# Sets of quarter-array matmuls placed one behind the other on TensorE, two pauses in the planner, and later batches planned two steps sooner

## The chip, the cores and the metric

The kernel runs on one core of one Trainium2 chip. The metric is the device time of one execution in microseconds (us), as the median of several runs; a profiled execution comes with a trace of every instruction. TensorE is called PE in the profile, VectorE DVE, ScalarE ACT, GpSimd POOL and SyncE SP; SP issues the DMAs.

## The reference

The input is `x` of 8 batches x 3136 tokens x 256 channels, with a filter of 1569 frequencies and two weight matrices of a two-layer product.

```
X = rfft(x, axis=1);  y = irfft(X * filter)               # along the 3136 tokens
mixed = real(fft(fft(y, axis=1), axis=2))                 # along tokens and channels
u = y + mixed
un = (u - mean(u)) / sqrt(var(u) + 1e-6)                  # along the channels
out = u + relu(un @ w_ch1) @ w_ch2                        # 256 -> 1024 -> 256
```

## The kernel before

All transforms are matrix products. A batch goes through these stages, each in seven parts: a first forward stage (`first_pair`, for batches 2 to 7), a second forward stage with the filter (`spectrum`), a transpose by DMA, a first inverse stage (`inverse1`), and a second inverse stage (`inverse2`), whose rows go to DRAM (`dy`) and come back in groups of 256 rows (`fetch`). For each of the 49 groups `prepare` mixes channels and normalizes, and `products` makes the two weight products. Numbers are kept as pairs of float16, so most products are three matmuls. One "step" is an eighth of a group: one piece of the first product (`h`, six matmuls of 512 columns, L1564) and two halves of the second (`acc`, six matmuls of 256 columns each, L1604), with everything else threaded between. There are 392 steps, and they keep TensorE in work from about 95 us to the end.

Three kinds of work use the array as four quarters of 64 x 64, each quarter with its own rows and its own output partitions, so that four matmuls run side by side. They are called sets here: an **s set** (`first_pair`, L671), an **i set** (`inverse1`, L1075, with L1066 in a batch's first part) and a **y set** (`inverse2`, L1198). A set takes two of the four PSUM banks of the ring `psf`; `spectrum` and `mixing` take one bank of the same ring each. All other matmuls use the whole array.

The order of all instructions on every engine is fixed when the kernel is built, by a planner (`Plan`). Each piece of work is a Python generator that yields an engine, an assumed length in us and, if wanted, a key; the planner keeps a clock of its own, lines the pieces up per engine (`line_up`) and, when an engine comes free (`run`), takes the one with the lowest key. On the chip the engines follow that order and wait on semaphores, so a piece that the planner thought ready and that is late holds up its engine. A "gate" at t lets a piece go on when step t - 4 is done (`gate`, L1283). Keys are in steps: the first product of step q has key q, the second q + 2.5. The s set has key t - 6 (`BOOST`, L667), the y set t - 8 (L1187), the i set t itself (L1062).

The scale of a batch (`weigh_x`, L610 to L626) is a maximum over measures of the seven pieces of `x` (L600, ScalarE, each after its load), a square root on ScalarE (L617), a transpose on TensorE (`pow2`, L470), a few operations on VectorE and a product with ones on TensorE (`spread`, L488). For the i set, `spectrum` ends in a DMA transpose issued by SP (L958), which writes `z`; after it `done("z", ...)` lets `inverse1` go on.

The time of a batch's stages hangs on one number, `brought(b, c)` (L1275), the step at which part c of batch b is wanted:

```python
return 8 * ((b * NS + 224 * c) // 256) - COME - (c == 1) * 2
```

`load_b2` (L1126) brings part c's input back from DRAM at a gate of `brought(b, c) - 3`, and `inverse2` (L1173) is gated at `brought(b, c)`. The main program sets the other stages back from `brought(b, 0)`: `s0` (spectrum) is `brought(b, 0) - 5.2 - 6.5 - 13 * 1.45`, `t0` (first stage) is `s0 - 4.6 - 13 * 1.15`, `x0` (loads of `x`) is `t0 - 8.5`, and the i set of part ch has t = `s0 + 1.45 * (2 * ch + 1) + 6.5`.

Of the kernel before, what the change touches and what calls it, by code (L numbers as in the profile page):

```python
# [26 lines left out]
NS = N // 2  # L27
# [7 lines left out]
COME = 18  # L35
# [4 lines left out]
TWIN = 0.86  # L40
FOURS = 0.85
BOOST = 6
PASSES = ((0, 0), (1, 0), (0, 1))
BACKED = 6.5
RAW_IN = (None, None, "ys", "ys", "ut", None, None, None)
# [20 lines left out]
class Plan:  # L66


    def __init__(self):
        self.now = self.end = self.moved = 0.0  # L70
        self.heap, self.count, self.live = [], 0, 0
        self.queues = {e: [] for e in ("PE", "DVE", "ACT", "POOL", "SP", "calm")}
        self.free_at = dict.fromkeys(self.queues, 0.0)

    def post(self, t, f, *args):
# [11 lines left out]
    def step(self, task, value, issued=None):  # L87
        try:
            what, *rest = task[0].send(value)
        except StopIteration:  # L90
            self.live -= 1
            return
        if issued is not None and what not in ("PE", "DVE", "ACT", "POOL"):
            self.end = issued
        if what in self.queues:
            if len(rest) > 1:
                task[1] = rest[1]
            self.post(self.end + HOP * (task[2] != what), self.line_up, what, task, rest[0])
            task[2] = what
        elif what == "until":  # L100
            self.until(task, list(rest))
        elif what == "take":
            self.post(self.end, self.ask, rest[0], task, *rest[1:])

# [9 lines left out]
    def set(self, event, now=False):  # L114
        end = self.end
        if now:
            self.end = self.now
        event.time = self.end
        for task, events in event.waiting:
            self.until(task, events)  # L120
        self.end = end

    def line_up(self, engine, task, length):
        self.count += 1
# [25 lines left out]
    def run(self):  # L150
        while self.heap:
            self.now, _, f, args = heapq.heappop(self.heap)
            f(*args)
            while self.heap and self.heap[0][0] <= self.now:
                _, _, f, args = heapq.heappop(self.heap)
                f(*args)
            for e, queue in self.queues.items():
                if e == "calm" and queue:
                    e = "SP"
                    if self.moved > self.now + CALM:  # L160
                        self.post(self.moved - CALM, int)
                        continue
                if queue and self.free_at[e] <= self.now:
                    _, _, task, length = heapq.heappop(queue)
                    if e == "SP":
                        issue = TURN if length == 1.65 else ISSUE
                        self.moved = max(self.moved, self.now + issue + REACH) + length
                        self.free_at[e] = max(self.now + issue, self.moved - BACKLOG)
                        self.end = self.moved + LANDED
                    else:  # L170
                        self.end = self.free_at[e] = self.now + length
                    self.post(self.free_at[e], int)
                    self.step(task, None, self.free_at[e] if e == "SP" else None)
        assert not self.live
# [199 lines left out]
def _program(ctx, tc, nc, a, NB):  # L374
# [22 lines left out]
    def give(name, *ks):  # L397
        for k in ks:
            plan.give(rings[name], k)
# [6 lines left out]
    def done(*key):  # L406
        plan.set(ev(*key))
# [55 lines left out]
    def pow2(col, name):  # L463

        rows = col.shape[0]
        ring, bank_ = ("psh", spare) if name in ("x0", "F") else ("psf", bank)
        k = yield take(ring)
        pt = bank_("pt_" + name)
        yield "PE", 0.3
        nc.tensor.transpose(pt[:1, :rows], col, ident[:rows, :rows])  # L470
        yield "DVE", 0.9
        row = tp.tile([1, 2], F32, tag="row", name="row_" + name, bufs=3)
        nc.vector.tensor_reduce(row[:, 0:1], pt[:1, :rows], axis=AX.X, op=ALU.max)
        give(ring, k)
        nc.vector.tensor_scalar(row[:, 0:1], row[:, 0:1], 1e-18, None, op0=ALU.max)
        ri = row.bitcast(I32)
        nc.vector.tensor_scalar(ri[:, 0:1], ri[:, 0:1], EXPO, None, op0=ALU.bitwise_and)
        nc.vector.tensor_scalar(ri[:, 1:2], ri[:, 0:1], EXPO, None, op0=ALU.bitwise_xor)
        return row
# [130 lines left out]
    def weigh_x(b):  # L610
        yield until(*(("mx", b, q) for q in range(7)))
        m = ms[b]
        yield "DVE", 0.2
        nc.vector.tensor_reduce(m[:, 7:8], m[:, 0:7], axis=AX.X, op=ALU.max)
        if b:
            yield "ACT", 0.25
            nc.scalar.activation(m[:, 7:8], m[:, 7:8], AF.Sqrt)  # L617
        row = yield from pow2(m[:, 7:8], f"x{b}")
        if b:
            yield "DVE", 0.3  # L620
            nc.vector.tensor_scalar(row[:, 0:1], row[:, 0:1], 1 / (16 * SMALL), None, op0=ALU.mult)
            nc.vector.tensor_scalar(row[:, 1:2], row[:, 1:2], 16 * SMALL, None, op0=ALU.mult)
        sx = tp.tile([128, 2], F32, tag="sx", name=f"sx_{b}", bufs=3)
        yield from spread(sx, row, f"x{b}")
        sxs[b] = sx
        done("sx", b)  # L626
# [30 lines left out]
    def first_pair(b, q, t):  # L657

        yield gate(t)
        yield until(("sx", b), ("s1q",))  # L660
        if b not in d1s:
            d1s[b] = dp.tile([2, 56, 28, 2, 256], F16, tag="d1", name=f"d1_{b}")
        x = xs[b, q]
        sx = sxs[b][:, 1:2]
        kp = yield take("psf", 2)
        ps = [bank(f"s1_{b}_{q}_{i}").rearrange("p (n c) -> p n c", n=2) for i in range(2)]
        yield "PE", FOURS, t - BOOST  # L667
        for c in range(2):
            for i in range(2):
                row = slice(64 * i, 64 * i + 56)  # L670
                nc.tensor.matmul(  # L671
                    ps[i][64 * c : 64 * c + 64], s1q[row], x[row, 2 * c : 2 * c + 2], start=True, stop=True
                )
        give("big", 21 * b + q - 7)
        kx = yield take("x16")
        odd = fp.tile([128, 2, 256], F32, tag="x16", name=f"odd_{b}_{q}", bufs=3)
        yield "ACT", 0.58
        nc.scalar.activation(odd, ps[1], AF.Copy, scale=sx)
        for out, op in ((ps[1], ALU.subtract), (odd, ALU.add)):
            yield "DVE", 0.73  # L680
            nc.vector.scalar_tensor_tensor(out, ps[0], sx, odd, op0=ALU.mult, op1=op)
        give("psf", kp)
        k = yield take("ast")
        st = fp.tile([128, 2, 2, 2, 256], F16, tag="ast", name=f"ast_{b}_{q}", bufs=3)
        yield "ACT", 0.55
        nc.scalar.copy(st[:, 1, :, 0], ps[1])
        plan.spawn(sum_half(b, q, kx, odd, st), t)
        yield "DVE", 0.66
        nc.vector.tensor_tensor(st[:, 1, :, 1], ps[1], st[:, 1, :, 0], op=ALU.subtract)
        give("psf", kp + 1)  # L690
        yield until(("sum", b, q))
        for c in range(2):
            yield "SP", 0.85
            n = 4 * q + 2 * c
            nc.sync.dma_start(
                d1s[b][:, :, n : n + 2].rearrange("s p n h c -> p s (n h c)"),
                st[64 * c : 64 * c + 56].rearrange("p s n h c -> p s (n h c)"),
            )
        give("ast", k)
        done("d1", b, 2 * q)  # L700
        done("d1", b, 2 * q + 1)
# [153 lines left out]
    def spectrum(b, ch, hf, t):  # L855
# [103 lines left out]
            zs[b, ch][:, :, 128 * hf : 128 * hf + 128], y16.rearrange("p l j q -> p (l j q)")  # L959
        )  # L960
        give(f"y16_{hf}", k)
        done("z", b, ch, hf)

    spectra, mixed = {}, [0]
# [89 lines left out]
    def inverse1(b, ch, t):  # L1054
# [4 lines left out]
        kp = yield take("psf", 2)  # L1059
        ps = [bank(f"i1_{b}_{ch}_{i}").rearrange("p (j c) -> p j c", j=2) for i in range(2)]  # L1060
        z = zs[b, ch].rearrange("p (l j) c -> p l j c", l=2)
        yield "PE", TWIN + 0.5 * (ch == 0), t - 0  # L1062
        if ch == 0:
            for s in range(2):
                for i, (lx, lw) in enumerate(PASSES):
# [3 lines left out]
        for i, (lx, lw) in enumerate(PASSES):  # L1069
            for jj in range(2):  # L1070
                for c in range(ch == jj == 0, 2):
                    e = 4 * ch + 2 * c + jj + 1
# [100 lines left out]
    def inverse2(b):  # L1173
        for c in range(1 - min(b, 1), 7):
            t = urgent(b, c)
# [8 lines left out]
            k, bt = b2s[b, c]  # L1184
            kp = yield take("psf", 2)
            ps = [bank(f"y_{b}_{c}_{o}").rearrange("p (j c) -> p j c", j=2) for o in range(2)]
            yield "PE", TWIN if b else 2 * TWIN, t - 8  # L1187
            passes = PASSES if b else [(0, None)]
            for i, (lx, lw) in enumerate(passes):
                table = i2[:, :, lw] if b else i2f  # L1190
                for js in range(2):
                    for o in range(2):
                        row = slice(64 * o, 64 * o + 56)
                        for h in range(2):
                            e, half, turn = 2 + 2 * h + js, h, js
                            if c == o == 0:
                                e, half, turn = h if js == 0 else 2 + 2 * h, js, h
# [76 lines left out]

    def brought(b, c):  # L1275

        return 8 * ((b * NS + 224 * c) // 256) - COME - (c == 1) * 2

    def urgent(b, c):

# [495 lines left out]
    for b in range(NB):  # L1776
# [23 lines left out]
        for ch in range(7):  # L1800
            for h in range(2):
                t = s0 + half * (2 * ch + h)
                plan.spawn(spectrum(b, ch, h, t), t)
            t = s0 + half * (2 * ch + 1) + 2.2
# [72 lines left out]
```

## Time and profile before

| what | value |
| --- | --- |
| time, three runs | 1388.2 us median (1386.5, 1388.2, 1391.54) |
| profiled execution | 1391.44 us, span 1389.6 us |
| mean granted TensorE clock | 0.992 |
| PE busy | 1354.4 us, 97% of the span |
| DVE, ACT, POOL busy | 72%, 61%, 51% of the span |
| chain that ended last | PE 72%, DMA 8%, DVE 7%, POOL 4%, ACT 4%, issue 3% |

Busy times are shares of the span from the first to the last instruction. In a timeline a row is a run of like instructions: its start, its length, the engine and line, what it writes and reads, and the count. The lengths of neighbouring matmul rows overlap, since matmuls are pipelined; the pace is read from the starts.

### The profile page before, as it was taken

The numbers are of one execution on the slowest core, as the hardware profiler recorded it, in microseconds if no ns is written. First come the engines' busy times: TensorE is split into PE (matmuls) and PEld (weight loads), VectorE is DVE, ScalarE is ACT, GpSimd is POOL, SyncE is SP. The second block draws the span as 40 slices with busy tenths as digits, with TensorE's granted clock in tenths as the row PEclk, the third lists the DMA queues.
The fourth block names the chain that finished last, engine by engine and source line by source line (L and its number), as shares of the span: only waits on it lengthen the run. The fifth ranks groups of instructions, "written<-read, shape, count | busy, mean of one in ns | idle before, by whom it ended". The sixth has DMA issues, their size and how long they took to land.

```text
span 1389.6 us, 33404 instructions
## 1 busy us (share of the span) xinstructions
PE 1354.4 (97%) x12879; PEld 917.6 (66%) x12879; DVE 997.1 (72%) x2162; ACT 845.3 (61%) x1631; POOL 706.4 (51%) x865
## 2 busy tenths in 40 slices
PE   9989999999899999999999999999899999999998
PEld 8845766666657765677656665666566776666666
DVE  6888896788678777678677875777648778465442
ACT  6776567556755677565765667647656565444341
POOL 2713881378536864388443863368614766222210
PEclk9989999999999999999999999999999999999999
DMA  9797998699889897887979797787966986554320
GB/s 259 238 249 209 240 202 208 204 227 205 195 231 238 184 199 192 256 188 185 228 197 217 174 218 182 216 205 170 221 176 180 205 197 168 141 138 105 100 61 31
DMA packets 353603, 265.35 MB, mean 191 GB/s; under 512 B 216188, under 2 KB 290588, under 8 KB 353444
## 3 DMA queue, kind: packets, MB, share of 16 engines
q1 hardware_dynamic: 353444, 263.22, 77.8%
q8 instruction: 101, 1.65, 0.5%
q14 instruction: 58, 0.48, 0.1%
HBM read 113.72 MB, written 99.09 MB: 153 GB/s over the span
## 4 chain that ended last, share of the span: by engine, by line
PE 72%; DMA 8%; DVE 7%; POOL 4%; ACT 4%; issue 3%; SPq 2%; DVEq 0%; POOLq 0%; ACTq 0%
PE acc L1604 29%; PE h L1564 29%; DMA x<-xq 4%; PE s L671 3%; PE y L1198 3%; PE s L890 2%; PE mix L1305 2%; PE i L1075 2%; DMA z<-late 1%; DMA ft<-fiT 1%; ACT xsq L600 1%; DVE h L1593 1%; DMA ft<-frT 1%; POOL eo L1011 1%; POOL late L954 1%
## 5 line engine op out<-in xcount | busy, mean ns | idle before, releaser
L1604 PE MATMUL acc<-w2s,h 128*128 128x256 f16 x4704 | 589.0, 273 | 1.2 <-ACT u L1529 1.0
L1564 PE MATMUL h<-ut,w1s 128*128 128x512 f16 x2352 | 575.6, 381 | 0.2 <-DVE ut L1521 0.2
L1604 PEld LDWEIGHTS <-h 128*128 128x128 f16 x4704 | 449.1, 98 | 138.9 <-issue 24.2
L1593 DVE SCALAR_TENSOR_TENSOR h<-h,h 128x512 f16<-128x512 f32 x392 | 267.8, 683 | 227.1 <-ACT h L1591 225.3
L1591 ACT ACTIVATE h<-h 128x512 f16<-128x512 f32 x392 | 232.8, 594 | 305.6 <-PE h L1564 303.6
L1564 PEld LDWEIGHTS <-w1s 128*128 128x128 f16 x2352 | 225.8, 98 | 205.9 <-issue 14.2
L1535 POOL TENSOR_TENSOR u<-un,u 128x512 f16<-128x512 f32 x92 | 106.4, 1157 | 222.5 <-ACT u L1529 186.5
L1355 POOL TENSOR_TENSOR pages<-sm,pages 128x508 f32<-128x508 f32 x49 | 62.0, 1266 | 107.0 <-ACT sm L1396 66.0
L1507 ACT ACTIVATE un<-pages,sb 128x256 f32<-128x256 f32 x196 | 109.0, 592 | 10.0 <-DVE sb L1454 8.9
L954 POOL TENSOR_TENSOR late<-yt,late 128x448 f16<-128x448 f32 x98 | 102.7, 1052 | 21.2 <-ACT late L952 19.8
L707 POOL TENSOR_TENSOR ast<-odd,ast 128x512 f16<-128x512 f32 x42 | 48.4, 1157 | 123.6 <-ACT ast L705 118.7
L1476 DVE BATCH_NORM_STATS2 st<-pages 128x6 f32<-128x256 f32 x196 | 80.6, 411 | 12.9 <-POOL pages L1361 11.2
L1330 DVE SCALAR_TENSOR_TENSOR pages<-mix,alpha,pages 128x254 f32<-128x254 f32 (+2 forms) x184 | 81.4, 476 | 9.0 <-ACT sm L1396 7.5
L909 DVE SCALAR_TENSOR_TENSOR yt<-s,pF,ft 128x448 f32<-128x448 f32 x98 | 66.0, 674 | 28.1 <-PE s L890 27.0
L1120 POOL TENSOR_TENSOR bt<-sd,bt 128x512 f16<-128x512 f32 x42 | 48.6, 1158 | 70.3 <-ACT bt L1118 70.0
L925 POOL TENSOR_TENSOR yt<-yt,t 128x224 f32<-128x224 f32 x98 | 64.6, 659 | 36.1 <-DVE t L909 33.7
L952 ACT CAST late<-yt 128x448 f16<-128x448 f32 x98 | 54.9, 562 | 40.0 <-POOL yt L927 39.5
L1224 ACT ACTIVATE ys<-y,alpha 128x512 f32<-128x512 f32 x98 | 62.2, 682 | 26.3 <-PE y L1198 22.3
L1618 DVE SCALAR_TENSOR_TENSOR pages<-acc,beta,pages 128x512 f32<-128x512 f32 x98 | 68.6, 741 | 7.3 <-PE acc L1604 7.2
L978 POOL TENSOR_TENSOR ef<-yt 128x224 f32<-128x224 f32 x112 | 72.6, 669 | 0.3
L1011 POOL TENSOR_TENSOR eo<-ef,eo 128x448 f16<-128x448 f32 (+6 forms) x62 | 59.7, 967 | 25.2 <-ACT eo L1007 16.9
L909 DVE SCALAR_TENSOR_TENSOR t<-s,pF,ft 128x448 f32<-128x448 f32 x98 | 65.9, 673 | 0.5 <-POOL yt L927 0.5
(191 smaller groups left out, 1676.6 us busy)
## 6 DMA issues: line engine op xcount, KB each, us to landing
pages<-d SPq DMA_DIRECT2D x112, 224.0 KB
out<-pages SPq DMA_DIRECT2D x98, 256.0 KB
pages<-dy SPq DMA_DIRECT2D x90, 256.0 KB
d<-ast SPq DMA_DIRECT2D x98, 224.0 KB
d<-bt SPq DMA_DIRECT2D x98, 224.0 KB
dy<-ys SPq DMA_DIRECT2D x96, 224.0 KB
x<-xq SPq DMA_DIRECT2D x42, 480.0 KB
at<-d SPq DMA_DIRECT2D x84, 224.0 KB
```

The costliest lines, as they stand in the source:

```text
L909: nc.vector.scalar_tensor_tensor(out, p, pF[:, 1:2], f, op0=ALU.mult, op1=ALU.mult)
L954: nc.gpsimd.tensor_tensor(y16v[:, 1], yh, y16v[:, 0], op=ALU.subtract)
L978: nc.gpsimd.tensor_tensor(eft[:, i], yt[:, 0, i], yt[:, 1, i], op=o)
L1011: nc.gpsimd.tensor_tensor(lo, efv[:, :, e0 : e0 + n], hi, op=ALU.subtract)
L1330: nc.vector.scalar_tensor_tensor(out, p, al, y, op0=ALU.mult, op1=ALU.add)
L1476: nc.vector.bn_stats(st[:, 2 * t + k], y[:, t, k])
L1507: nc.scalar.activation(un[:, k], y[:, t, k], AF.Identity, bias=sb[:, i, 1:2], scale=sb[:, i, 3:4])
L1535: nc.gpsimd.tensor_tensor(u16[:, :, :, 1], unv, u16[:, :, :, 0], op=ALU.subtract)
L1564: nc.tensor.matmul(p.rearrange("p (t k q) -> p t k q", t=2, k=2), w1s[:, d, hw, 128 * f : 128 * f + 128], utv[:, :, :, d, hx], start=i == ...
L1591: nc.scalar.activation(h[:, 0], p, AF.Relu)
L1593: nc.vector.scalar_tensor_tensor(h[:, 1], p, 0.0, h[:, 0], op0=ALU.max, op1=ALU.subtract)
L1604: nc.tensor.matmul(acc[:, kind], h[:, hh, c0 : c0 + 128], w2s[:, f, hw], start=f == 0 and kind == 0 and i == 0, stop=f == 7 and kind == 1 ...
```

## The change

Five edits, all in the planner and in what is yielded to it. No instruction is added or removed.

- The three kinds of sets are lined up in a queue of their own, "quarters", which TensorE serves beside its other queue. When both hold work and the last piece was not a set, the lower key goes first, as before; when the last piece was a set, a set that is lined up goes first whatever its key. A set that follows a set is counted 0.2 us shorter (`MERGED`).
- `weigh_x` waits 1.5 us of planner time before the transpose of the scale is lined up, for batches 2 to 7.
- `spectrum` waits 1 us of planner time behind the DMA transpose, before `z` is called done, for batches 2 to 7.
- For batches 3 to 7 `brought` is two steps lower.
- For the same batches parts 2, 4 and 6 get the `brought` of parts 1, 3 and 5.

```diff
@@ class Plan, __init__, step @@
-        self.queues = {e: [] for e in ("PE", "DVE", "ACT", "POOL", "SP", "calm")}
+        self.queues = {e: [] for e in ("PE", "DVE", "ACT", "POOL", "SP", "calm", "quarters")}
+        self.in_quarters = False
+        elif what == "pause":
+            self.post(self.end + rest[0], self.resume, task, None)
@@ class Plan @@
+    def on_tensor(self):
+
+        whole, quarters = self.queues["PE"], self.queues["quarters"]
+        if whole and quarters and not self.in_quarters:
+            return min(whole, quarters)
+        return quarters or whole
@@ run @@
+                if e == "quarters":
+                    continue
+                if e == "PE":
+                    queue = self.on_tensor()
                 if queue and self.free_at[e] <= self.now:
                     _, _, task, length = heapq.heappop(queue)
+                    if e == "PE":
+                        small = queue is self.queues["quarters"]
+                        length -= MERGED * (small and self.in_quarters)
+                        self.in_quarters = small
@@ weigh_x @@
+        if b > 1:
+            yield "pause", 1.5
         row = yield from pow2(m[:, 7:8], f"x{b}")
@@ first_pair, inverse1, inverse2 @@
-        yield "PE", FOURS, t - BOOST
+        yield "quarters", FOURS, t - BOOST
-        yield "PE", TWIN + 0.5 * (ch == 0), t - 0
+        yield "quarters", TWIN + 0.5 * (ch == 0), t - 0
-            yield "PE", TWIN if b else 2 * TWIN, t - 8
+            yield "quarters", TWIN if b else 2 * TWIN, t - 8
@@ spectrum @@
         give(f"y16_{hf}", k)
+        if b > 1:
+            yield "pause", 1
         done("z", b, ch, hf)
@@ brought @@
-        return 8 * ((b * NS + 224 * c) // 256) - COME - (c == 1) * 2
+        if b > 2 and c:
+            c -= (c - 1) % 2
+        return 8 * ((b * NS + 224 * c) // 256) - COME - (c == 1) * 2 - 2 * (b > 2)
```

## Rows read from the trace of the kernel before

**Rows 1.** The page's part 1: engine, busy us, share of the span, instructions.

```profile
PE 1354.4 (97%) x12879; PEld 917.6 (66%) x12879; DVE 997.1 (72%) x2162; ACT 845.3 (61%) x1631; POOL 706.4 (51%) x865
```

**Rows 2.** Waits of TensorE from 95 us on: total us, times, longest us.

```profile
PE i L1075 <- DMA z<-late: 7.7, 3, 6.4
PE pt_x L470 <- ACT mx L617: 6.5, 4, 2.8
```

**Rows 3.** The timeline of TensorE: the first and the last set.

```profile
79.43 1.09 PE L1198 MATMUL y<-pages,i2f 56*64 56x256 f32 x16
...
1304.70 0.85 PE L1198 MATMUL y<-pages,i2f 56*64 56x256 f16 x24
```

**Rows 4.** The timeline of TensorE, 798 to 809 us: start us, us, work.

```profile
800.26 0.84 PE L1198 MATMUL y<-pages,i2f 56*64 56x256 f16 x22 [0.24 <-DVE t L909]
...
802.77 1.46 PE L1564 MATMUL h<-ut,w1s 128*128 128x512 f16 x6
804.06 0.82 PE L1604 MATMUL acc<-w2s,h 128*128 128x256 f16 x6
...
805.79 1.46 PE L1564 MATMUL h<-ut,w1s 128*128 128x512 f16 x6
807.18 0.85 PE L1075 MATMUL i<-z,late 56*64 56x256 f16 x24
807.96 1.27 PE L1604 MATMUL acc<-w2s,h 128*128 128x256 f16 x10
```

**Rows 5.** The same view around 417 us, where two sets stand together.

```profile
415.82 1.46 PE L1564 MATMUL h<-ut,w1s 128*128 128x512 f16 x6
417.20 1.50 PE L1198 MATMUL y<-pages,i2f 56*64 56x256 f16 x48
418.64 1.48 PE L1604 MATMUL acc<-w2s,h 128*128 128x256 f16 x12
```

**Rows 6.** TensorE's groups by line, first 807.1 us, then first 634.0: xcount, busy, mean ns.

```profile
L1564 PE MATMUL h<-ut,w1s 128*128 128x512 f16 x1254 | 307.5, 381 | 0.2 <-DVE ut L1521 0.2
...
L1564 PE MATMUL h<-ut,w1s 128*128 128x512 f16 x942 | 231.6, 382 | 0.2 <-DVE ut L1521 0.2
```

**Rows 7.** Timelines of SP: the second transposes of the two sets in Rows 4 and 9.

```profile
795.53 1.23 SPq L958 DMA_TRANSPOSE z<-late  x1
...
612.46 1.24 SPq L958 DMA_TRANSPOSE z<-late  x1
```

**Rows 8.** The chain that ended last, around 473 and 998 us: start us, us, what.

```profile
472.94 3.10 DMA z<-late
...
998.37 9.87 DMA z<-late
```

**Rows 9.** The timeline of TensorE, 622 to 636 us.

```profile
631.22 0.85 PE L1198 MATMUL y<-pages,i2f 56*64 56x256 f16 x24
...
634.06 0.85 PE L1075 MATMUL i<-z,late 56*64 56x256 f16 x24
```

**Rows 10.** The page's part 5: the eviction of a y set's two banks.

```profile
L1224 ACT ACTIVATE ys<-y,alpha 128x512 f32<-128x512 f32 x98 | 62.2, 682 | 26.3 <-PE y L1198 22.3
```

**Rows 11.** The timeline of TensorE around 491 us: an i set after its first matmul.

```profile
491.25 0.85 PE L1075 MATMUL i<-z,late 56*64 56x256 f16 x23 [1.49 <-DVE bt L1099]
```

**Rows 12.** Timelines of TensorE, 376 to 381, then 853 to 862 us: scale's transpose.

```profile
378.27 0.26 PE L470 MATMUL pt_x<-ident,mx 120*1 120x120 f32 x1 [1.62 <-ACT mx L617]
...
856.54 0.26 PE L470 MATMUL pt_x<-ident,mx 120*1 120x120 f32 x1 [2.82 <-ACT mx L617]
```

**Rows 13.** Engines by stretch: us, busy of PE, PEld, DVE, ACT, POOL; granted clock, DMA share, GB/s.

```profile
856.67:860.08 3.41, 3.41 (x16) 2.05 (x15) 1.88 (x8) 3.38 (x7) 2.04 (x2) 0.50 0.29 70
1001.90:1008.28 6.38, 0.01 (x1) 0.00 (x0) 4.63 (x11) 4.50 (x10) 4.98 (x6) 0.89 1.05 238
1008.28:1013.68 5.40, 5.40 (x40) 3.32 (x41) 0.00 (x0) 1.15 (x2) 0.00 (x0) 0.50 1.12 290
```

**Rows 14.** The timeline of TensorE, 1001 to 1015 us.

```profile
1008.28 1.49 PE L1075 MATMUL i<-z,late 56*64 56x256 f16 x24 [6.38 <-DMA z<-late]
```

More of the change, by code (lines that the diff above doesn't have):

```diff
@@ L42 @@
 BOOST = 6
+MERGED = 0.2
 PASSES = ((0, 0), (1, 0), (0, 1))
@@ L92, in step @@
             return
-        if issued is not None and what not in ("PE", "DVE", "ACT", "POOL"):
+        if issued is not None and what not in ("PE", "DVE", "ACT", "POOL", "quarters"):
             self.end = issued
```

## The prediction

> **What bounds the kernel now.** I read the page's busy shares first: TensorE is busy for 97% of the span, the next engine for 72% [rows 1]. So the time is TensorE's work plus its waits, and nothing that only relieves another engine shows. Next, the waits of TensorE behind the start-up: two kinds are large, the i set on the DMA that transposes `z` (7.7 us, three times) and the scale's transpose on ScalarE's square root (6.5 us, four times) [rows 2]. Then the timeline, by starts, for what a set costs beyond its own matmuls. Last the granted clock in the stretches right behind the long waits. The last set starts at 1304.70 [rows 3], 85 us ahead of the end, and behind it TensorE has products only; so a stage that ends sooner doesn't by itself end the kernel sooner.
>
> **Sets that follow one another.** A piece `h` takes 1.29 us from its start to the next piece's (802.77 to 804.06) [rows 4]. With an i set behind it, `h` starts at 805.79 and the work after the set at 807.96, 2.17 us: the set costs 2.17 - 1.29 = 0.88 us [rows 4]. Where two y sets stand together it is 418.64 - 415.82 - 1.29 = 1.53 us for both [rows 5], so the second costs 0.65 and a set that joins another saves about 0.23; I use 0.22. There are 42 s sets, 49 i sets, and 55 y sets by the code; counted along the timeline they stand in 124 runs, the first and the last of them in [rows 3], so 22 of the 146 already have a set ahead of them.
>
> How many more will join? s and y sets have keys 6 and 8 steps below their time, under any product's key, so before the change too they went as soon as they were lined up: for them the new queue alone does almost nothing. It is i sets, with key t, that sit in line while their data are there. Example: part 3 of batch 5 has t = 222 - 30.55 + 10.15 + 6.5 = 208.1 and ran when 1254 / 6 = 209 pieces `h` (steps 0 to 208) were done [rows 6], to the step when its key came up. Its second transpose was issued at 795.53 [rows 7]; with the 3.1 us that such a transfer took at 473 us [rows 8] it had landed at 798.6, before the y set of 800.26 [rows 4]. The change would draw it in behind that set. Of the 42 i sets of batches 2 to 7, I count 15 that start at the step of their key like this one, and 9 of these have a set ahead of them in that time.
>
> Others are later than their key though their data are long there. Part 1 of batch 4 (key 174 - 30.55 + 4.35 + 6.5 = 154.3) ran after 942 / 6 = 157 pieces [rows 6], at 634.06, with its transpose issued at 612.46 [rows 7], which lands by 622.4 even with the longest transfer of the chain, 9.9 us [rows 8]. A y set ran at 631.22, and 2 us behind its end this set [rows 9]. What it waited for is a pair of banks; such sets don't join. The same limit meets the second idea: parts 1 and 2, 3 and 4, 5 and 6 of batches 3 to 7 (15 pairs of y sets) now fall due together, but the second needs the other two banks at once. I take 6 of the 15. So 15 joins, 15 x 0.22 = **3.3 us**, with bounds of 5 (1.1 us) and 30 (6.6 us).
>
> The trace shows the eviction as the longer part: ScalarE takes 682 ns for each of a y set's two banks [rows 10], 1.36 us against the 0.88 of the set, and one i set stood for 1.49 us behind its first matmul until VectorE had cleared its second bank [rows 11]. The Trainium skill's page "TensorEngine Tiling (Array Packing)", section Performance Considerations, says that tiling speeds up TensorE but not the emptying of PSUM. It speaks against this change; by it no pair forms beyond those of before, and the sum would lose its 3.3 us.
>
> **The pause before the scale's transpose.** The pause adds no instruction; the transpose, and behind it the product with ones and the first s set, stand 1.5 us later in TensorE's order, with products ahead of them as cover. It takes off up to 1.5 us from each of the four waits: 1.5 each from 1.62 and 2.82 us [rows 12], and the other two, 6.5 - 1.62 - 2.82 = 2.0 together, whole: 5.0 us. Behind the 2.82 us wait the granted clock was 0.50, the level of 1.2 GHz, for 3.41 us in which TensorE was busy throughout [rows 13]; half of that, 1.7, was lost. Behind the 1.62 us wait there is no such stretch. With 1.3 us of it left I count the 1.7 too: **6.7 us** (bounds 0, if each transpose is just as late against its new place, and 6.5 + 1.7 = 8.2).
>
> **The pause behind the transpose of `z`.** Two waits of 1.3 us together go, and 1.0 of the long one, 6.38 us at 1008 [rows 14]: **2.3 us**. The remaining 5.4 us and the clock behind it, 0.50 over 5.40 us of work [rows 13], 2.7 us lost, I leave in: its transfer took 9.87 us [rows 8] while the DMA engines were full (share 1.05) [rows 13], which a pause of 1 us doesn't cover. Bounds 0 and 7.7 + 2.7 = 10.4.
>
> **Two steps sooner.** A step is 173.1 us / 52 = 3.33 us [rows 6]. For batches 3 to 7 the loads of `x`, the s sets, spectra, transposes, i sets and y sets move together by 6.7 us, so they keep their distances; SP issues the same DMAs sooner, ahead of groups' `fetch` and `out` transfers that stay. By the formula the y sets of part 2 move by 12 steps, those of parts 4 and 6 by 10 in most batches, and with them their two loads each and their `dy` stores: part 2's loads now fall just behind the batch's last transposes, where the next batch's `x` loads are. In itself I cost it at nothing, with products as cover.
>
> **New waits.** An i set drawn in ahead of its key gives up slack: some would find `z` still on its way. Without any slack three sets waited 7.7 us in all [rows 2]; the pause covers the short ones. I charge 2.0 us (bounds 0 and, one more wait like the long one, 6.4 us).
>
> **The sum.** -3.3 - 6.7 - 2.3 + 2.0 = -10.3 us. Against the profiled execution's own time, 1391.4, that is 1381.1. The median of the runs is 1388.2, 3.2 lower, in all likelihood with a shorter long wait, of which the sum takes only 1.0; I carry the difference over: **1378 us**. What is late next is TensorE's own work.
>
> **The rivals.** (1) *The sets don't join*, since banks are held: for it the late i sets above, against it the pair at 417 us. Then 5 joins: 1388.2 - 1.1 - 6.7 - 2.3 + 2.0 = 1380. (2) *The waits come back elsewhere*: the planner makes a new order everywhere, and a chain (load of `x`, measure, root) that is late on the chip is late against any place. Only the joins stay: 1388.2 - 3.3 = 1385, no change. For it: two of six batches wait for nothing and one 2.8 us, so lateness scatters. Against it: a fixed pause shortens every wait. (3) *Slower: the sooner loads meet the transposes.* Place: the end of each batch's inverse stage, where the DMA engines are full already [rows 13]. Price of one such wait: 6.4 + 2.7 = 9.1 us. One more of them eats the gain (1387); from two more on it decides: 1378 + 18 = 1396; of seven batches one has it now. The Trainium skill, "Trainium Kernel Development and Optimization", Key Constraints, says that all DMAs share the same 16 engines and interleave; the share of 1.05 agrees.
>
> **How the numbers follow.** About 0.5% (7 us) is what a measurement of this kernel can tell from no change: faster is below 1381.3, slower above 1395.1. The forecast has 0.60 (0.52 of it below 1381.3), rival 1 0.13 (0.08 below), rival 2 0.18 (0.02 below), rival 3 0.09 (0.07 above 1395.1, the rest between). Faster 0.62, same 0.31, slower 0.07. Lowest, with the good bounds: 1388.2 - 6.6 - 8.2 - (10.4 - 3.2) = 1366. At the top the range takes in rival 2 and one more long wait: 1389. Outside lie most of rival 3 and a little of the rest.
>
> **What would show it.** Joins: rows of 48 matmuls y or of y and i next to each other, and fewer than 110 runs. The pause: idle time before L470 below 2 us in all. `z`: no short waits before L1075. Rival 2: the same sum of TensorE's waits under other names. Rival 3: waits of 4 us and more before L1075 or L1198 on a DMA, with a granted clock of 0.50 behind them. I'd be wrong most easily about the number of joins and the long waits.

## The result and the profile after

| | before | after |
| --- | --- | --- |
| median | 1387.99 us (6 runs, 1386.5 to 1391.54) | 1401.09 us (6 runs, 1397.52 to 1405.09) |
| ratio, 95% interval | | 1.0089 (1.0067 to 1.0111) |
| profiled execution, span | 1391.44, 1389.6 us | 1401.35, 1399.6 us |

The change makes the kernel 13 us slower where 10 us of gain were forecast. One run of e3 below, of 2315.57 us, was in a slow state and is left out of e3's median, which would be 1416.8 us with it (the 1417 of later expectations). The page of after begins as that of before [rows 1]: TensorE is busy for 97% of the span, and only 4 us longer in all.

```profile
span 1399.6 us, 33390 instructions
...
PE 1358.3 (97%) x12879; PEld 923.8 (66%) x12879; DVE 1005.3 (72%) x2162; ACT 844.5 (60%) x1631; POOL 706.0 (50%) x865
```

TensorE's waits from 95 us on (total us, times, longest) show what was traded. The scale's transpose (now L489) waits 0.8 us instead of 6.5 [rows 2]: that pause did its work. The i sets (now L1098, with L1089 in a batch's first part) wait for the transposes of `z` 19.8 us in nine waits, instead of 7.7 in three.

```profile
PE i L1098 <- DMA z<-late: 17.5, 7, 4.4
PE i L1089 <- DMA z<-late: 2.3, 2, 2.0
PE y L1221 <- DMA pages<-d: 1.8, 3, 0.8
...
PE pt_x L489 <- ACT mx L636: 0.8, 1, 0.8
```

Behind five of the waits the granted clock is lower, as it was behind two before [rows 13]. By stretch (us, busy of the engines, clock, DMA share, GB/s), each from the end of a wait:

```profile
376.02:380.60 4.58, 4.58 (x38) 3.05 (x39) 2.59 (x7) 2.81 (x6) 1.15 (x1) 0.50 0.76 181
464.53:469.40 4.87, 4.87 (x58) 4.02 (x58) 2.42 (x4) 2.44 (x7) 1.95 (x4) 0.65 1.21 289
505.46:513.73 8.27, 8.27 (x86) 5.09 (x87) 3.89 (x7) 4.35 (x9) 2.88 (x5) 0.79 1.06 217
534.48:537.60 3.12, 3.12 (x33) 2.13 (x34) 0.19 (x1) 1.76 (x4) 3.00 (x5) 0.50 1.13 236
681.40:684.40 3.00, 3.00 (x28) 1.63 (x28) 0.00 (x0) 0.00 (x0) 0.89 (x1) 0.50 1.13 303
```

A clock of 0.50 is the level of 1.2 GHz; the stretches at 0.65 and 0.79 hold work at both levels. Length times the missing share is 2.3 + 1.7 + 1.7 + 1.6 + 1.5 = 8.8 us lost, against 1.7 + 2.7 = 4.4 before. All waits of the view together are 26.5 us against 19.2. Counted along the timeline, sets stand in 118 runs against 124, which saves 6 x 0.22 = 1.3. So waits +7.3, clock +4.4, joins -1.3: +10.4 us; the spans differ by 10.0. The start-up, in which both programs have the same order up to 170 us, took 2.8 us longer in this execution of after; with it the sum is 13.2, and where 3 us were won back I can't say.

**How one of the waits comes about.** After's timeline of SP around 500 us (start us, us, work):

```profile
499.22 2.20 SPq L979 DMA_TRANSPOSE z<-late  x1
```

its timeline of TensorE there:

```profile
500.66 1.47 PE L1629 MATMUL acc<-w2s,h 128*128 128x256 f16 x12
505.46 0.85 PE L1098 MATMUL i<-z,late 56*64 56x256 f16 x24 [3.32 <-DMA z<-late]
```

and the chain that ended last there (start us, us, what):

```profile
499.22 6.11 DMA z<-late
```

The issue of the transpose ends at 501.42. The i set comes to the head of TensorE at 505.46 - 3.32 = 502.14, 0.7 us behind that. The transfer lands at 505.33. The planner put the set behind the end of the *issue*, not behind the landing. The reason is in `step` (L89 to L107 of after):

```python
if issued is not None and what not in ("PE", "DVE", "ACT", "POOL", "quarters"):
    self.end = issued                                   # end of the DMA's issue
...
elif what == "pause":
    self.post(self.end + rest[0], self.resume, task, None)
```

When SP's piece is taken, `run` sets `self.end` to the landing and hands the end of the issue to `step` as `issued`. Before, the generator went straight on to `done("z", ...)` and set the event at the landing. With the pause the next thing it yields is none of the engines in the tuple, so its clock is set back to the end of the issue, and the 1 us runs from there. By the planner's own constants (`REACH` 0.5, length 1.65, `LANDED` 1.5; at most `BACKLOG` 4.5 + 1.5) the landing lies 3.65 to 6.0 us behind the end of the issue. So on the planner's clock the pause calls `z` done 2.65 to 5 us *sooner* than before. The pause of the scale stands behind a piece on ScalarE, where `issued` is None, and does what it says. This is theory I below; the runs test it.

### The profile page after: what moved, and what is told of

Read it like the earlier page. It is cut to its first block, busy times and chain, and to the rows that moved or that the text cites. A ratio compares the mean times of both kernels' runs of the same rounds, so it can differ in the third digit from the quotient of the medians.

```text
span 1399.6 us, 33390 instructions
## 1 busy us (share of the span) xinstructions
PE 1358.3 (97%) x12879; PEld 923.8 (66%) x12879; DVE 1005.3 (72%) x2162; ACT 844.5 (60%) x1631; POOL 706.0 (50%) x865
## 3 DMA queue, kind: packets, MB, share of 16 engines
q8 instruction: 101, 1.65, 0.5%
## 4 chain that ended last, share of the span: by engine, by line
PE 69%; DMA 10%; POOL 8%; DVE 7%; ACT 3%; issue 2%; SPq 1%; DVEq 0%; POOLq 0%; ACTq 0%
PE acc L1629 28%; PE h L1589 28%; DMA z<-late 5%; PE s L692 3%; PE y L1221 2%; PE mix L1330 2%; PE i L1098 2%; PE s L911 2%; POOL late L975 1%; DMA ft<-fiT 1%; POOL yt L948 1%; POOL u L1560 1%; DVE h L1618 1%; DMA pages<-d 1%; POOL yt L946 1%
```

## The experiments

All times are medians, with the 95% interval of the ratio to the kernel before, which ran beside each (medians 1387.95 to 1389.07 us). Theories: Q, i sets drawn in by the queue lose their slack; S, the sooner stages put transfers where the transposes are; I, the pause calls `z` done too early; N and N2, the rest of the change, or any pause there, makes the waits; R, any new order of the plan scatters by several us; C and D, a pair of parts is to blame. "Runs" counts runs of sets (124 before).

| kernel | us | ratio | waits on z, us (times) | scale's transpose, us | runs |
| --- | --- | --- | --- | --- | --- |
| before | 1388.0 | 1 | 7.7 (3) | 6.5 | 124 |
| after | 1401.1 | 1.0067 to 1.0111 | **19.8 (9)** | 0.8 | 118 |
| e1 queue alone | 1384.6 | 0.9951 to 0.9986 | 2.3 (3) | 7.1 | 121 |
| e2 scale pause alone | 1387.9 | 0.9982 to 1.0009 | 2.4 (3) | 0.4 | 125 |
| e3 z pause alone | 1414.8 | 1.0169 to 1.0237 | **27.1 (7)** | 4.2 | 123 |
| e4 sooner stages alone | 1379.1 | 0.9902 to 0.9954 | 0.6 (2) | 4.2 | 121 |
| f1 all but z pause | 1393.6 | 1.0025 to 1.0061 | 7.9 (4) | 1.3 | 124 |
| f2 all, z pause from landing | 1391.8 | 1.0015 to 1.0040 | 9.1 (4) | 0 | 121 |
| f3 all, z pause 4 us | 1381.6 | 0.9909 to 0.9963 | 7.8 (5) | 0 | 118 |
| f4 z pause from landing alone | 1385.0 | 0.9962 to 0.9990 | 0.8 (2) | 3.8 | 123 |
| g1 queue, sooner | 1386.9 | 0.9973 to 1.0016 | 5.9 (4) | 3.7 | 124 |
| g2 scale pause, sooner | 1379.9 | 0.9927 to 0.9966 | 5.5 (4) | 0.9 | 124 |
| g3 queue, scale pause | 1394.8 | 1.0035 to 1.0078 | 8.9 (3) | 0.5 | 124 |
| c1 before, constant 0.11 | 1398.2 | 1.0051 to 1.0098 | 14.8 (4) | 3.4 | 125 |
| h1 constant 0.11, z pause | 1402.2 | 1.0083 to 1.0126 | **20.6 (7)** | 0 | 126 |
| h2 before, constant 0.09 | 1391.9 | 1.0012 to 1.0035 | 2.8 (3) | 5.4 | 126 |
| h3 after, constant 0.11 | 1412.1 | 1.0117 to 1.0215 | **29.9 (10)** | 0.8 | 123 |
| h4 as h3, z pause from landing | 1387.0 | 0.9975 to 1.0009 | 2.2 (2) | 0.3 | 121 |
| h5 z pause alone, 4 us | 1402.4 | 1.0066 to 1.0134 | 18.0 (4) | 1.8 | 123 |
| h6 sooner, z pause from landing | 1382.6 | 0.9939 to 0.9977 | 1.8 (1) | 3.1 | 116 |

Three of the waits counted as waits on `z` stand in the profile under another DMA: 1.7 us in e2 (`dy<-ys`), 0.6 in f2 and 6.7 in c1 (`x<-xq`). An i set reads nothing of what those DMAs move. In each case that DMA shares a semaphore with one of the set's transposes, and in the trace a transpose of `z` that the set needs ends within 0.15 us of the wait's end.

**One part at a time.** e1 to e4 are the kernel after with the other three parts taken out, by these edits:

```diff
@@ no queue: first_pair, and so inverse1 and inverse2 @@
-        yield "quarters", FOURS, t - BOOST
+        yield "PE", FOURS, t - BOOST
@@ no scale pause @@
-        if b > 1:
-            yield "pause", 1.5
@@ no z pause @@
-        if b > 1:
-            yield "pause", 1
@@ no sooner stages @@
-        if b > 2 and c:
-            c -= (c - 1) % 2
-        return 8 * ((b * NS + 224 * c) // 256) - COME - (c == 1) * 2 - 2 * (b > 2)
+        return 8 * ((b * NS + 224 * c) // 256) - COME - (c == 1) * 2
```

> The queue for sets alone: no pauses, no sooner stages. Theory Q (a set drawn in ahead of its key gives up the slack that hid the transfer of z): slower by 8 to 13 us, 1396 to 1401, with most of the 20 us of TensorE's waits on z already here. Theory S (the sooner stages and paired parts put transfers where the transposes are): about 1385, some 10 sets joined and waits on z like before's 8 us. If the sets hardly join (118 to 122 runs of sets), the queue does nothing by itself: 1386 to 1390.

> Only the pause of 1.5 us before the scale's transpose, batches 2 to 7. By both theories the waits before the transpose on the square root fall from 6.5 to under 1 us; the time falls by 5 to 7 us to 1381 to 1383 if nothing else moves. A rival R (any new order of the plan moves the waits on z by several us either way): the waits on z leave the 8 us of before by more than 4 us, though nothing about z was changed.

> Only the pause of 1 us behind the DMA transpose of z, batches 2 to 7. If the plan is late by a fixed small amount, the waits on z fall from 8 us to 5 or less, time 1383 to 1387. Rival R: they change by more than the pause explains, up or down, and the scale's waits too.

> Only the times of batches 3 to 7: two steps sooner, and parts 2, 4, 6 with parts 1, 3, 5. Theory S: slower by 8 to 13 us, 1396 to 1401, with waits on z of 15 us or more. Theory Q: 1385 to 1391, waits on z near 8 us; a few y sets stand in pairs.

Q and S fall: the queue alone is 3.4 us and the sooner stages 8.8 us faster. A loss, of 27 us, is in the part that I had priced as a gain of 2.3 us. The same three views of e3 around 1010 us show the picture of after, larger. SP:

```profile
1006.04 1.23 SPq L977 DMA_TRANSPOSE z<-late  x1
```

TensorE:

```profile
1006.50 0.85 PE L1096 MATMUL i<-z,late 56*64 56x256 f16 x24
1016.45 1.50 PE L1096 MATMUL i<-z,late 56*64 56x256 f16 x24 [9.10 <-DMA z<-late]
```

The chain:

```profile
1006.04 10.37 DMA z<-late
```

The issue ends at 1007.27, the next i set is at TensorE's head at 1007.35, and the transfer takes 10.37 us. It is part 5 of batch 6, next to the set behind the 9.87 us of before [rows 8], which is part 6, the batch's last; the next batch's `x` loads are ahead of it in the queue.

e2 is a warning of its own. The scale's waits went from 6.5 to 0.4 us as forecast, and the time stayed: one new wait of 7 us, with a slow stretch behind it, stands elsewhere, on the transpose of a product's input. The timeline of TensorE in e2:

```profile
754.45 2.72 PE L1585 MATMUL h<-ut,w1s 128*128 128x512 f16 x6 [6.96 <-DMA ut<-u]
756.97 2.34 PE L1625 MATMUL acc<-w2s,h 128*128 128x256 f16 x12
```

Its waits on `z` fell as well, from 7.7 to 2.4 us, though nothing about `z` was changed. That is what R expected. The two rows that make them up (total us, times, longest), the first under the other DMA's name:

```profile
PE i L1096 <- DMA dy<-ys: 1.7, 1, 1.7
...
PE i L1096 <- DMA z<-late: 0.7, 2, 0.5
```

**The pause's count.** f1 leaves the z pause out of the change, as above. f2 counts it from the landing, by this edit; f4 has the same edit and only this pause. f3 has `yield "pause", 4` there.

```diff
-        if issued is not None and what not in ("PE", "DVE", "ACT", "POOL", "quarters"):
+        if issued is not None and what not in ("PE", "DVE", "ACT", "POOL", "quarters", "pause"):
```

> The whole change but the pause behind the transpose of z. Theory I (in the planner a task that yields a pause right behind a DMA issue goes on from the end of the issue, not from the landing, so the pause of 1 us calls z done several us too early): the waits on z fall from 20 us to under 5, the time to 1372 to 1382, faster than before. Rival N (the joins and the sooner stages together make the waits on z): 1395 or more, waits on z above 12 us.

> The whole change, but the planner counts the pause of 1 us from the landing. Theory I: waits on z under 4 us, 1372 to 1382. Rival N2 (any pause in that place hurts, since the i set keeps its place in line with banks or the z pages longer): 1395 or more. The pause from the landing should be within 4 us of the kernel without that pause.

> The whole change with 4 us for 1 us behind the transpose. Theory I: counted from the issue, 4 us is near what a transfer takes when the DMA engines are not full (3.1 us) and short of the long ones (10 us): the waits on z fall to between 3 and 10 us, the time to 1376 to 1392. Rival N2: a longer pause is worse, above 1401.

> The kernel before with only the pause behind the transpose, counted from the landing. Theory I: the 27 us of waits on z of the same kernel with the pause counted from the issue are gone (under 6 us), time 1381 to 1389. Rival N2: 1400 or more, as with the other count.

f4 against e3 is the cleanest pair: the same pause, one word in a tuple apart, 1385.0 against 1414.8 us, and 0.8 us of waits on `z` against 27.1. N2 falls. The waits of e3, then of f4 and of f1 (total us, times, longest):

```profile
PE i L1096 <- DMA z<-late: 26.8, 6, 9.1
...
PE i L1087 <- DMA z<-late: 0.3, 1, 0.3
```

```profile
PE i L1096 <- DMA z<-late: 0.8, 2, 0.4
```

```profile
PE i L1096 <- DMA z<-late: 7.9, 4, 4.7
```

But f1 and f2, at 1393.6 and 1391.8, are neither the 1372 to 1382 of theory I nor the 1395 of N, and their waits on `z`, 7.9 and 9.1 us, are above the 5 and 4 that theory I wanted: without the early `z` the rest of the change still lost 4 to 6 us here, though each of its parts alone had lost nothing. f3 came out inside its range, 1381.6 us with 7.8 us of waits on `z`. So f1 and f3 have the same waits on `z` and stand 12 us apart; all waits of TensorE are 22.2 us in f1 and 14.3 in f3.

**Which pair?** g1 to g3 put two parts together, by the edits of e1 to e4; c1 is the kernel before with one constant of the planner changed, the time that it counts for a hand-over from one engine to the next.

```diff
-HOP = 0.1
+HOP = 0.11
```

> Queue for sets and sooner stages, no pause. If the parts add, 1388 - 3.4 - 8.8 = 1376. Theory C (the pause before the scale's transpose, with the sooner stages, shifts the first stage of one batch against the inverse stage of the one before, and costs the 5 us by which the change without the z pause is still slower): 1374 to 1381. Theory D (the queue and the sooner stages together cost it): 1388 to 1396. Theory R (any new order scatters by several us, no pair is to blame): anywhere in 1376 to 1392.

> The pause before the scale's transpose and the sooner stages, without the queue and without the z pause. If the parts add, 1379. Theory C: 1388 to 1396, with waits at the ends of batches 2 and 3 (360 to 380 and 520 to 540 us). Theory D: 1376 to 1381. Theory R: anywhere between.

> Queue for sets and the pause before the scale's transpose, no sooner stages and no z pause. If the parts add, 1384. If this pair alone costs what remains: 1390 to 1396. Theories C and D: 1381 to 1388.

> The kernel before with one constant of the planner, the time that it counts for going from one engine to the next, 0.11 us for 0.10: a new order without any of the change's edits. Theory R: the time leaves 1388 by 3 us or more, and the waits of TensorE behind 95 us stand in other places. If orders scatter little: 1386 to 1390.

No one pair explains it. g2 kept the gain of the sooner stages and g1 lost it. g3 is 6.8 us slower than before, out of parts that gained 3.4 and 0: that is the range it was to have if this pair costs what remains, but g1, without the scale's pause, falls about as far short of its sum (11 us against 10). Both hold the queue; yet f3, and h4 below against c1, hold it too and are fast, so the queue isn't shown to cost it either. c1 shows that no pair need be to blame. A hundredth of a us in a constant that has nothing to do with the change costs 10 us, three quarters of what the whole change cost. Its waits of TensorE (total us, times, longest) hold a large one that the profile puts down to a load of `x`:

```profile
PE i L1075 <- DMA z<-late: 8.1, 3, 4.0
PE i L1075 <- DMA x<-xq: 6.7, 1, 6.7
```

The set is part 5 of batch 2. Its two transposes were issued at 344.44 and 349.55 us, and the load shares a semaphore with the first. The second, in the timeline of SP,

```profile
349.55 3.06 SPq L958 DMA_TRANSPOSE z<-late  x1
```

sent its last update at 364.06 us in the trace, 14.5 us behind its start, and the set began at 364.10. So this too is a wait on `z`, without any pause: the new order put a set where a transfer was slow. In TensorE's timeline it has a slow stretch behind it (a piece `h` takes 2.54 us by the starts, not the 1.29 of [rows 4]):

```profile
364.10 1.50 PE L1075 MATMUL i<-z,late 56*64 56x256 f16 x24 [6.75 <-DMA x<-xq]
365.52 2.74 PE L1564 MATMUL h<-ut,w1s 128*128 128x512 f16 x6
368.06 1.99 PE L1604 MATMUL acc<-w2s,h 128*128 128x256 f16 x12
```

So the sum of parts can't be tested by adding medians of single edits: each is one draw of an order.

**The same parts in other orders.** h1, h3 and h4 have the constant at 0.11, h2 at 0.09. h5 is e3 with 4 us, h6 is e4 with the pause of f4.

> The planner's constant at 0.11 (1398 us by itself) and the z pause of 1 us, counted from the issue as in the change. Theory I (the pause calls z done too early, whatever the order): waits on z of 18 us or more, 1405 or slower. Theory R alone (the 1417 of the z pause in the first order was that order's scatter): 1380 to 1400, waits on z near 8 us.

> The kernel before with the planner's constant at 0.09: a second order without any of the change's edits, for the scatter. Theory R: between 1378 and 1400, again away from 1388 by 3 us or more.

> The whole change with the constant at 0.11. Theory I: again slower than before, 1393 to 1410, waits on z of 15 us or more. Theory R alone: as likely below 1388 as above.

> The whole change with the constant at 0.11 and the z pause counted from the landing. Theory I: faster than the same with the pause from the issue by 6 us or more, waits on z lower by 8 us or more. Theory R alone: either sign.

> The kernel before with only the z pause, 4 us for 1, counted from the issue. Theory I: z is called done 3 us later than with 1 us (1417), about when a transfer lands while the DMA engines are not full, too early at a batch's end: waits on z of 3 to 15 us, well under 27; 1383 to 1400. Theory R alone: no relation to the 1 us case.

> The two parts that gained alone: sooner stages and paired parts (1379), and the z pause of 1 us counted from the landing (1385); no queue, no scale pause. If they add: 1376; with the scatter that the planner's constant showed: 1372 to 1392. Waits on z under 4 us in any case by theory I.

Waits on `z` of h3 (both lines of the i set), then of h4, which differs from it in that tuple alone:

```profile
PE i L1098 <- DMA z<-late: 22.8, 6, 6.0
PE i L1089 <- DMA z<-late: 7.1, 4, 2.7
```

```profile
PE i L1098 <- DMA z<-late: 2.2, 2, 1.3
```

h3 against h4 is 1412.1 against 1387.0 us. h3 is 2 us above its range, on the side of theory I. h1 came out short of its 1405 and only 4 us behind c1, since c1 is a bad order itself, with 14.8 us of waits on `z`; h1's 20.6 are where theory I put them, but its interval overlaps that of c1, so this pair shows little. h5 missed: 4 us from the issue, about the planner's own estimate of a landing and up to 2 us short of it where the queue is full, is no better than 1 us there (18.0 us of waits, the longest 7.2), while in f3 it was harmless. The planner's estimate, at most 6.0 us behind the end of the issue, is short of the longest transfers in either case; whether an i set stands there is the order's luck. So the dependence on the pause's length isn't settled. The waits of h5:

```profile
PE i L1096 <- DMA z<-late: 18.0, 4, 7.2
```

h6 has few waits on `z`, as expected, and doesn't add the two gains up.

Over all kernels the two groups don't overlap, though c1 comes near. In the four kernels with `z` called done 1 us behind the issue the waits on `z` are 19.8, 20.6, 27.1 and 29.9 us, and the times 1401 to 1415. In the 14 where it is called done at the planner's landing or 1 us behind it, they are 0.6 to 9.1 us, but for the 14.8 of c1, and the times 1379 to 1398. f3 and h5, with 4 us, are one on either side.

## Why the prediction was wrong, step by step

**The pause behind the transpose of `z`: wrong sign, and the step that failed.** The prediction took 1 us from each wait and set the lower bound at 0. It read "pause" as counted from the landing and didn't follow `step` with a task that has just issued a DMA, though the tuple that decides it was in the diff. Measured: waits on `z` up by 12 us in the profile, and in pairs that differ by the pause or its count alone, after against f1 +7.5, after against f2 +9.3, e3 against f4 +30, h3 against h4 +25 us; h1 against c1, +4, isn't clear of noise. The term needed a bound on the side of a loss: a pause moves the point in the plan at which the i set is let go, and that can be sooner. Of the 23 us between forecast and result it holds 2.3 + 7.5 = 9.8, by f1. Without it the forecast would still have missed: f1 stands 13 us above the 1380 that is left of it, for the reasons below.

**The scale's pause: right in place, lost in the sum.** The prediction wanted idle time before the transpose below 2 us; it is 0.8 us, and 0 to 1.3 in the eight other kernels with that pause; in the eleven without it 1.8 to 7.1, but for h1 with none. The 6.7 us didn't reach the end: e2 is 1387.9, with a new wait of 7 us elsewhere. That is the outcome of rival 2, a wait taken off and no time won, but not by the chain it named: the scale's transpose was no longer late, and what came was a wait on `ut`. All waits of e2 are 15.3 us against 19.2. Whether the pause or the scatter of orders made the wait on `ut` isn't shown.

**The joins: mechanism right, far too many.** A join is worth what was worked out [rows 4, 5]; but of 15 wanted, 6 came (118 runs), and e1, the queue alone, made 3 (121). Even kernels without the queue range from 116 to 126. y sets of paired parts do stand together, four times in after, five in e4, for which the sooner stages are enough, as here in e4:

```profile
1220.22 1.46 PE L1585 MATMUL h<-ut,w1s 128*128 128x512 f16 x6
1221.61 1.50 PE L1217 MATMUL y<-pages,i2f 56*64 56x256 f16 x48
1223.04 1.16 PE L1625 MATMUL acc<-w2s,h 128*128 128x256 f16 x9
```

It costs 1223.04 - 1220.22 - 1.29 = 1.53 us, as in [rows 5]. Rival 1 was the truer case for this part. That held banks are the cause was argued from the rows, and no run tried it.

**Two steps sooner: costed at nothing.** Alone it is 8.8 us faster, and g2 and h6 with it are faster too; g1 isn't. Rival 3, which made this part the loser, had the right kind of wait (an i set on its DMA, with a slow clock behind it) and a price of 1396 near the 1401 measured, but the wrong cause, and it wanted two more long waits where many shorter ones came: one of nine is above 4 us. Why it gains isn't shown beyond its short waits on `z` in e4 (0.6 us); with a scatter of several us between orders it may be partly luck.

**New waits: 2.0 us, of the wrong kind.** The term was priced from the slack of i sets drawn in, and nothing of that shows: waits on `z` are 2.3 us in e1 and 7.9 in f1, against 7.7 before. What the runs show in its place is the scatter of the whole order: kernels with nothing but a constant changed took 1391.9 and 1398.2. The range, 1366 to 1389, should have gone up by about 10 us for this alone. f3, the whole change with a pause of 4 us, came to 1381.6, near the forecast; next to f1 with the same waits on `z` that is an order's luck and no support for the sum. f1 has waits that before has not, among them 3.9 us of a product on the transpose of its input; why the order of f1 has them stays open.

Of the kernels run, e4 is the fastest, 1379.1 us, 0.7% faster than before (0.9902 to 0.9954): the sooner stages and paired parts without the queue and the pauses.

## What to carry to other kernels

In a kernel whose order comes from a planner, a wait put into the plan is an edit of the plan's model of time: follow the planner's clock through the very piece that stands ahead of it, above all a DMA, whose issue ends long before its landing. Before an edit of such a kernel is believed to gain or lose under one per cent, change a constant that should do nothing and see how far the time moves; an edit is then tested in two orders or more, and by the waits it is meant to change rather than by the time alone. A wait taken off one engine is worth its length only if the profile shows that the same time doesn't return under another name. And where the profile has an instruction wait for a DMA whose data it doesn't read, as in c1, look for the transfer it does read.

## What the runs showed of the hardware

The end of a DMA transpose's issue tells little of its landing: an issue of 1.23 us went with a landing 10.37 us behind its start while `x` loads were under way (e3), one of 3.06 us with 14.5 us (c1), and the first of two that took 2.95 us together with 3.10 us at another place [rows 8]. By the updates of their semaphores in the trace of before, its 98 transposes of `z` landed 2.7 to 13.6 us behind their start, the median 4.0. In the profile of after the granted clock was 0.50 for about 3 to 5 us behind waits of 2.7, 3.8 and 4.4 us alike, so such a wait cost its length and 1.5 to 2.3 us more.
